# A fused attention and feed-forward kernel: part of the first v on a second queue, and the second batch's q and k loaded and transposed earlier

## The chip, the cores and the metric

The kernel runs on one core of one Trainium2 chip. The metric is device time in microseconds (us); lower is better. Before the change the median of three runs is 308.27 us (307.86 to 308.33). The profile shown here is of one execution that took 307.91 us, of which 306.1 us lie between its first and its last instruction. TensorE's granted clock was 1.000 throughout.

## What is computed

Sliding-window attention for 8 batches of 8 heads, sequence length 576, head dimension 64, then a feed-forward layer over all 4608 tokens with a quadratic-linear activation (smelu). Cut to what matters:

```python
def _attn_ref(q, k, v):                       # q, k, v: (8, 8, 576, 64) fp32
    scores = 1/sqrt(64) * q @ k^T
    scores = where(abs(i - j) <= 32, scores, -1e9)
    attn = softmax(scores)
    return attn @ v

def _moe_ref(x, w_in, w_out):                 # x (4608, 512), w_in (512, 2048), w_out (2048, 512)
    h = x @ w_in
    g = where(h >= 1, h, where(h <= -1, 0, (h + 1)**2 / 4))
    return g @ w_out                          # (4608, 512) fp32

x = attn_out.transpose(0, 2, 1, 3).reshape(4608, 512)
return _moe_ref(x, w_in, w_out)
```

## The kernel before

The program is one long list of **slots** `a`. Slot `a` projects 256 tokens through 256 columns of `w_in` (eight matmuls into the PSUM tile `hp`), and evaluates the activation into `gT`. Eight slots make one block of 256 tokens. Around the slots lie the products of finished blocks with `w_out` (`pair` for the first blocks, `unit` later) and the attention of the batch that comes next: transposes of q and k, scores, `exp`, sums and normalisation into `xT`. Each slot's order on the engines is the order in which the program issues it:

```python
for a in range(NF * NB + 2 * NF):
    eng = None if a < 14 else V
    post = [] if a >= 40 else [x for n, x in pairs if n == a] + [a - NF] * (a >= 2 * NF + 2)
    ...
    hps = [pool.tile([128, 2, TB], FP, name="hp", tag=tag)]
    project(hps[0], f, r0, [(j, kk) for j in range(2) for kk in (0, 2, 1, 3)], True, True)
    ...
    rr = ewp.tile([128, 2, TB], FP, name="rr")
    A.activation(rr, hp, AF.Relu, scale=0.5, bias=0.5)
    mx = ewp.tile([128, 2, TB], FP, name="mx")
    if a in two_on_act:                       # two operations on ScalarE, one on VectorE
        A.activation(mx, rr, AF.Square)
        V.scalar_tensor_tensor(g, hp, 1.0, mx, op0=ALU.max, op1=ALU.min)
    else:                                     # one on ScalarE, two on VectorE
        V.tensor_max(mx, hp, rr)
        V.scalar_tensor_tensor(g, rr, 1.0, mx, op0=ALU.min, op1=ALU.mult)
    flush()                                   # the multiplications that normalise sums
    run(a)                                    # what at(a, ...) has put there
    for x in post:
        pair(x)                               # or unit
    ...
    run(a + 0.5)
```

`ewp` has three buffers for each name, so the `mx` of slot `a` uses the buffer of slot `a - 3`. `hp` has two PSUM buffers; slot 6 alone takes one from another pool.

What is planned for the first slots:

```python
pairs = [(6, 0), (7, 1), (8, 2), (9, 3), (11, 4), (12, 5), (15, 6), (15, 8), (16, 7), (17, 9)]
two_on_act = (1, 7, 8, 9, 10, 11, 12)
at(1, (tposes, 0, (0, 1), (1, 1)))                     # first batch, second half of q and k
at(2, (scores, 0, (0, 1), (0, 2), (2, 4)), (scores8, 0, ps_o))
at(3, (scores, 0, (1, 2), (0, 2), (2, 4), ps_n), (sums, 0, 0, TB, MAIN, ps_s))
at(4, (sums, 0, 1, TB, MAIN))
at(5, (sums, 0, 0, MAIN, S, ps_s))
at(13, seq[0][1])                                      # second batch, scores
at(13.5, (*seq[1][1], ps_n))
at(14, (*seq[0][0], ps_s), seq[1][0])                  # second batch, sums
...
for t in range(2):
    at(11 + t, (tposes, 1, (t, 0), (t, 1)))            # second batch, q and then k
```

`pair(x)` multiplies a quarter of the inner dimension of `w_out` (`g = x % 4`) for 256 output columns; `x` 0 to 3 therefore need the four quarters of `w_out` in turn.

The transposes of one `tposes` call go to two PSUM buffers, and the copies out of them are shared between two engines:

```python
def tposes(b, *sets):
    todo = []
    for (t, half), pool in zip(sets, (ps_s, ps_n)):
        tp = pool.tile([128, 2, 8, 128], BF, name="tp", tag="bb")
        todo += [tpose(b, 2 * half + part, t, (A.copy, V.tensor_copy)[part], tp[:, part]) for part in range(2)]
    for copy in todo:
        copy()
```

All inputs but the very first q are loaded by the GpSimd queue, which turns fp32 into bf16 on the way. v comes in rows of one head and token, 64 numbers. A tile of v holds 18 **chunks** of 64 tokens for each of four pairs of heads (nine of one head and nine of the next), and is loaded by four transfers:

```python
def load_v(b, n):
    ...
    nc.gpsimd.dma_start(out=vn[b][64 * a:64 * a + 64, :, h], in_=v[b, y:y + 2]
                        .rearrange("y s d -> (y s) d").rearrange("(c r) d -> r c d", r=64))
```

The order of the loads: first q (sync and ScalarE queues), then on the GpSimd queue the first half of k, v, and

```python
cuts = [0, 256, 512, 768, 1024, 1280, 1792, DFF]
w = [(load_w_in, c0, c1, h) for c0, c1 in zip(cuts, cuts[1:]) for h in range(2)]
put(w[:4] + [(load_half, 1, t, h) for t in range(2) for h in range(2)] + w[4:12])
put([(load_w_out, 0, 0, 4)] + w[12:])
put([(load_w_out, 0, k, k + 4) for k in range(4, 16, 4)] + [(load_rows, 1, t) for t in range(2)])
put([(load_v, 1, n) for n in range(4)])
...
put([(load_w_out, 1, 8 * n, 8 * n + 8) for n in range(2)])
put([(load_nat, 2, t) for t in range(2)] + [(load_v, 2, n) for n in range(4)])
```

Eight such transfers can be under way at once; each further one waits for the one issued eight before it.

Of the kernel before, what the change touches and what calls it, by code (L numbers as in the profile page):

```python
# [7 lines left out]
FP = mybir.dt.float32  # L8
# [6 lines left out]
def kernel(  # L15
# [19 lines left out]
    nc = tc.nc  # L35
    B, H, S, D = q.shape
    NT, DM, DFF = out.shape[0], 512, 2048
    NY = H // 2
    NC = S // 64
# [4 lines left out]
    PAD = 32  # L44
    WIDE = 72, 136
    LONG = 2

    const = ctx.enter_context(tc.tile_pool(name="const", bufs=1))
    nat = ctx.enter_context(tc.tile_pool(name="nat", bufs=2))
# [3 lines left out]
    ewp = ctx.enter_context(tc.tile_pool(name="ewp", bufs=3))  # L53
    osp = ctx.enter_context(tc.tile_pool(name="osp", bufs=3))
    ps_h = ctx.enter_context(tc.tile_pool(name="ps_h", bufs=2, space=bass.MemoryType.PSUM))
    ps_s = ctx.enter_context(tc.tile_pool(name="ps_s", bufs=1, space=bass.MemoryType.PSUM))
    ps_n = ctx.enter_context(tc.tile_pool(name="ps_n", bufs=1, space=bass.MemoryType.PSUM))
# [17 lines left out]
    V, P, A = nc.vector, nc.gpsimd, nc.scalar  # L75


    qn, kn, vn = {}, {}, {}
# [20 lines left out]
            nc.gpsimd.dma_start(out=x[:, :, h], in_=src[b, NY * h:NY * h + NY].rearrange("y s d -> (y s) d")  # L99
                                .rearrange("(u p) d -> p u d", p=128))  # L100

    def load_v(b, n):
        if b not in vn:
            vn[b] = nat.tile([128, 2 * NC, 2, D], BF, name="vn", tag="vn", bufs=3)
        h, a = divmod(n, 2)
        y = NY * h + 2 * a
        nc.gpsimd.dma_start(out=vn[b][64 * a:64 * a + 64, :, h], in_=v[b, y:y + 2].rearrange("y s d -> (y s) d")  # L107
                            .rearrange("(c r) d -> r c d", r=64))

    def load_w_in(c0, c1, h):  # L110
        nc.gpsimd.dma_start(out=w_in[64 * h:64 * h + 64, :, c0:c1],  # L111
# [32 lines left out]
    def put(todo):  # L144
        for fn, *x in todo:
            fn(*x)
# [2 lines left out]
    w = [(load_w_in, c0, c1, h) for c0, c1 in zip(cuts, cuts[1:]) for h in range(2)]  # L149
    put(w[:4] + [(load_half, 1, t, h) for t in range(2) for h in range(2)] + w[4:12])  # L150
    put([(load_w_out, 0, 0, 4)] + w[12:])
    put([(load_w_out, 0, k, k + 4) for k in range(4, 16, 4)] + [(load_rows, 1, t) for t in range(2)])
    put([(load_v, 1, n) for n in range(4)])
    P.tensor_copy(band[HD[1], 0:128], band[HD[1], 64:192])
    for m, n, x in ((mask4, 8, 128), (mask8, 4, TAIL)):
# [8 lines left out]
    def qkT(b, t):  # L164
        if t == 0:
            return qTs[b % 3][:, PAD:]
        if b not in kT:
            kT[b] = ktp.tile([128, NY * S], BF, name="kT")
        return kT[b]

    def tpose(b, n, t, copy, ps):


        half, part = divmod(n, 2)
        j0, j1 = ((0, 5), (5, 9))[part]
        if b:
            src = qn[b] if t == 0 else kn[b]
            src = [src[:, half + 2 * h] for h in range(2)]
            dst = qkT(b, t).rearrange("d (y e p j) -> d y e p j", y=2, e=2, j=9)[:, half, :, :, j0:j1]
            like = "d j (e p) -> d e p j"  # L180
        else:
            src = (qn, kn)[t][b, half]
            src = src if src.shape[1] == 9 else [src[:, h] for h in range(2)]
            dst = qkT(b, t).rearrange("d (y l p j) -> d l y p j", l=2, p=32, j=9)[:, half, :, :, j0:j1]
            like = "d j (p y) -> d y p j"
        for j in range(j0, j1):
            if isinstance(src, list):
                for h in range(2):
                    nc.tensor.transpose(ps[HD[h], j - j0], src[h][:, D * j:D * j + D], ident)  # L189
            else:  # L190
                nc.tensor.transpose(ps[:, j - j0], src[:, j], ident)
        return lambda: copy(dst, ps[:, :j1 - j0].rearrange(like, p=64 if b else 32))
# [120 lines left out]
    def flush():  # L313
        while muls:
            muls.pop(0)()


    TB = 256
# [6 lines left out]
    def tposes(b, *sets):  # L325

        todo = []
        for (t, half), pool in zip(sets, (ps_s, ps_n)):
            tp = pool.tile([128, 2, 8, 128], BF, name="tp", tag="bb")
            todo += [tpose(b, 2 * half + part, t, (A.copy, V.tensor_copy)[part], tp[:, part]) for part in range(2)]  # L330
        for copy in todo:
            copy()

# [14 lines left out]
    with tc.tile_pool(name="ps_p", bufs=1, space=bass.MemoryType.PSUM) as ps_p:  # L348
        keep_warm(11, ps_h, "hp")

        V.memset(qkT(0, 0).rearrange("d (y s) -> d y s", y=NY)[:, :, S // 2:352], 0.0)
        for b in range(LONG):
            V.memset(qkT(b, 0).rearrange("d (y s) -> d y s", y=NY)[:, :, S - PAD:], 0.0)
# [24 lines left out]

    NB = NT // TB
    NF = DFF // 256  # L380
    pairs = [(6, 0), (7, 1), (8, 2), (9, 3), (11, 4), (12, 5), (15, 6), (15, 8), (16, 7), (17, 9)]
    two_on_act = (1, 7, 8, 9, 10, 11, 12)
    ev = {}

    def at(a, *todo):


        ev.setdefault(a, []).extend(x for x in todo if x)

    def steps(b, cut):  # L390

        for k, (lo, hi) in enumerate(((0, cut), (cut, MAIN))):
            for y1 in range(2):
                yield (sums, b, y1, lo, hi), (scores, b, (y1, y1 + 1), (0, 2), (2 * k, 2 * k + 2))
        yield (sums, b, 0, MAIN, S), (scores8, b)
# [4 lines left out]
    at(4, (sums, 0, 1, TB, MAIN))  # L400
    at(5, (sums, 0, 0, MAIN, S, ps_s))
    seq = [x for b in range(1, B) for x in steps(b, 224)]
    at(13, seq[0][1])
    at(13.5, (*seq[1][1], ps_n))
    at(14, (*seq[0][0], ps_s), seq[1][0])
    at(16, seq[2][1])
    for n, a in enumerate((18, 20, 26.5, 28)):
# [5 lines left out]
    for n, a in enumerate(sl):  # L413
        at(a, seq[6 + n][0], seq[7 + n][1] if n < len(sl) - 1 else None)
    for t in range(2):
        at(11 + t, (tposes, 1, (t, 0), (t, 1)))
    loads, xps = {}, {16: [(2, 0)], 18: [(2, 1)]}
    for b in range(LONG + 1, B):
        a = sl[5 * (b - 1) - 7] - 17
# [7 lines left out]
    def home(t):  # L427

        return (3 - t % 4 if t % 4 in (0, 3) else t % 4) if WIDE[0] <= NF * t < WIDE[1] else t % 4
# [43 lines left out]
    def run(pos):  # L473
        todo = []
        for fn, *x in ev.get(pos, []):
            if fn is sums:
                todo.append(sums(*x))
            elif fn is tposes:
                tposes(*x)
            else:  # L480
                pool = (x.pop(),) if x[-1] in (ps_s, ps_n, ps_o) else ()
                fn(*x, eng, *pool)
        for end in todo:
            end()
# [10 lines left out]
    for a in range(NF * NB + 2 * NF):  # L495
        wide = WIDE[0] <= a < WIDE[1]
        eng = None if a < 14 else V
        post = [] if a >= 40 else [x for n, x in pairs if n == a] + [a - NF] * (a >= 2 * NF + 2)
        for b, x in loads.get(a, []):
            if x < 2:  # L500
                load_nat(b, x)
            else:
                for n in range(4):
                    load_v(b, n)
        if a == 0 or a > 3:
            flush()
        if a < NF * NB:
            if wide:
                n, f = divmod(a - WIDE[0], 2 * NF)
                t = WIDE[0] // NF + 2 * n  # L510
                r0 = TB * t % RING
                hp = ps_h.tile([128, 2, TB], FP, name="hp", tag="hp")
                for n, kk in enumerate((0, 2, 1, 3)):
                    nc.tensor.matmul(hp.rearrange("p n t -> p (n t)"), w_in[:, kk, 128 * f:128 * f + 128],  # L514
                                     xT[:, kk, r0:r0 + 2 * TB], start=n == 0, stop=n == 3)
                g = gT[:, f, home(t):home(t + 1) + 1:home(t + 1) - home(t)]
            else:
                t, f = divmod(a, NF)
                r0 = TB * t % RING
                if a in (0,):  # L520
                    hps = [ps_h.tile([128, 2, TB], FP, name="hp", tag="hp") for _ in range(2)]
                    for y in range(2):
                        for n in range(2):
                            project(hps[n], f + n, r0, [(j, y + 2 * m) for j in range(2) for m in range(2)], y == 0, y == 1)
                elif not hps:
                    pool, tag = (ps_o, "op") if a == 6 else (ps_h, "hp")
                    hps = [pool.tile([128, 2, TB], FP, name="hp", tag=tag)]
                    project(hps[0], f, r0, [(j, kk) for j in range(2) for kk in (0, 2, 1, 3)], True, True)
                hp = hps.pop(0)
                g = gT[:, 2 * f:2 * f + 2, home(t)]  # L530

            rr = ewp.tile([128, 2, TB], FP, name="rr")
            A.activation(rr, hp, AF.Relu, scale=0.5, bias=0.5)  # L533
            mx = ewp.tile([128, 2, TB], FP, name="mx")
            if a in two_on_act:
                A.activation(mx, rr, AF.Square)
                V.scalar_tensor_tensor(g, hp, 1.0, mx, op0=ALU.max, op1=ALU.min)
            else:
                V.tensor_max(mx, hp, rr)  # L539
                V.scalar_tensor_tensor(g, rr, 1.0, mx, op0=ALU.min, op1=ALU.mult)  # L540
        flush()
        run(a)
        for x in post:
            if x < 16:
                pair(x)
            else:
                for j in range(4):
                    unit(4 * x + j)
        if a >= 40:
            n = (4, 3, 3)[a % 3] if a < 88 else 4  # L550
            for x in range(done, done + n):
                unit(x)
            done += n
        run(a + 0.5)
        for x in xps.get(a, []):
            xpose(*x)

# [29 lines left out]
```

The softmax here doesn't subtract the row's maximum and nothing guards it: scores larger than these inputs give would overflow.

## Time and profile before

| | |
|---|---|
| Time, median of 3 runs | 308.27 us |
| Span of the profiled execution | 306.1 us |
| TensorE (PE) busy | 298.4 us |
| TensorE idle up to 44 us | 4.35 us |
| VectorE (DVE) busy, ScalarE (ACT) busy | 239.6 us, 191.2 us |
| Bytes moved by DMA | 35.67 MB, 117 GB/s on average |

In the time-ordered rows below, the first number is the start in us from the beginning of the span, the second is how long the row lasted, then come engine, source line, operation, and output<-inputs with partitions x elements. "x8" means that eight instructions are merged in the row. What stands in brackets at the end is how long the engine had been idle before the row and what released it. PEld is TensorE's weight load, which overlaps its matmuls. A row of POOL with the operation DMA_DIRECT2D is GpSimd writing the descriptors of a transfer, not the transfer itself. In a list of waits, the numbers after the colon are the total, how often, and the longest.

The projections start at the following times (slot: us): 0: 13.24, 2: 18.53, 3: 20.23, 4: 22.18, 5: 23.84, 6: 25.23, 7: 26.99, 8: 28.73, 9: 30.48, 10: 32.23, 11: 33.59, 12: 36.57, 13: 39.55, 14: 41.78, 15: 43.93. A projection takes 0.87 us where others follow it without a gap, as does one `pair`; a set of transposes takes 1.12.

### The profile page before, as it was taken

How to read it: one execution, taken by the hardware profiler on the slowest of the kernel's cores; microseconds unless marked ns; L12 is line 12 of the kernel's file. 1: busy time of each engine (PE TensorE's matmuls, PEld its weight loads, DVE VectorE, ACT ScalarE, POOL GpSimd, SP SyncE). 2: the span in 40 equal slices, each digit the busy share in tenths (PEclk: the TensorE clock that was granted, in tenths of full speed). 3: DMA queues.
4: the chain of work that ended last, by engine and by line, in shares of the span. 5: the costliest groups of instructions: out<-in, count | busy, mean ns of one | idle time of the engine just before them, and what ended most of it. 6: DMA issues, size and time to landing. Idle time of an engine off the chain costs nothing.

```text
span 306.1 us, 7974 instructions
## 1 busy us (share of the span) xinstructions
PE 298.4 (97%) x3388; PEld 181.2 (59%) x3388; DVE 239.6 (78%) x376; ACT 191.2 (62%) x320; POOL 77.1 (25%) x92
## 2 busy tenths in 40 slices
PE   8889999999999999999999999999999999999995
PEld 3468878876666676666654544444445444446644
DVE  3268568888888989998999998888888888788700
ACT  3688896748856856776766766665667654444311
POOL 8787661037009009004600900000000000000000
PEclk9999999999999999999999999999999999999999
DMA  9999999999999999999998991550101000000121
GB/s 153 184 197 198 186 196 153 173 156 164 139 186 109 181 169 124 165 144 116 148 127 166 145 156 39 111 115 34 36 34 37 36 34 35 36 34 34 59 80 69
DMA packets 137171, 35.67 MB, mean 117 GB/s; under 512 B 122160, under 2 KB 132912, under 8 KB 137136
## 3 DMA queue, kind: packets, MB, share of 16 engines
q0 software_dynamic: 102976, 18.06, 83.5%
q1 hardware_dynamic: 34016, 16.81, 26.1%
q8 instruction: 26, 0.43, 0.6%
q10 hardware_dynamic: 144, 0.29, 0.3%
q14 instruction: 9, 0.07, 0.1%
HBM read 36.70 MB, written 9.44 MB: 151 GB/s over the span
## 4 chain that ended last, share of the span: by engine, by line
PE 91%; POOL 3%; DMA 2%; ACT 1%; issue 1%; DVE 0%; POOLq 0%; ACTq 0%
PE op L449 36%; PE hp L489 22%; PE hp L514 18%; PE bb L295 6%; PE op L464 4%; PE bb L229 2%; DMA w_in<-in_moe_w_in_dram 2%; POOL vn L107 1%; PE op L440 1%; POOL w_in L111 1%; PE tp L189 1%; ACT pt L237 1%; POOL kh L86 1%; POOL qh L86 0%; PE bb L208 0%
## 5 line engine op out<-in xcount | busy, mean ns | idle before, releaser
L533 ACT ACTIVATE rr<-hp 128x512 f32<-128x512 f32 x144 | 85.5, 595 | 86.1 <-PE hp L514 41.7
L449 PE MATMUL op<-w_out,gT 128*128 128x512 bf16 x496 | 126.9, 380 | 0.0
L539 DVE TENSOR_TENSOR mx<-hp,rr 128x512 f32<-128x512 f32 x137 | 94.4, 689 | 26.1 <-ACT rr L533 24.3
L540 DVE SCALAR_TENSOR_TENSOR gT<-rr,mx 128x512 bf16<-128x512 f32 x137 | 94.8, 692 | 4.7
L489 PE MATMUL hp<-xT,w_in 128*128 128x256 bf16 x640 | 83.1, 273 | 2.2 <-DMA w_in<-in_moe_w_in_dram 1.4
L489 PEld LDWEIGHTS <-w_in 128*128 128x128 bf16 x640 | 61.8, 98 | 22.7 <-issue 2.8
L449 PEld LDWEIGHTS <-gT 128*128 128x128 bf16 x496 | 46.1, 98 | 45.2
L514 PE MATMUL hp<-xT,w_in 128*128 128x512 bf16 x256 | 65.7, 379 | 0.0
L514 PEld LDWEIGHTS <-w_in 128*128 128x128 bf16 x256 | 25.0, 98 | 30.2
L99 POOL DMA_DIRECT2D qn<-in_q_dram x12 | 14.6, 1224 | 89.5 <-DMA kT<-kn 87.4
L237 ACT ACTIVATE pt<-bb 128x1024 bf16<-128x1024 f32 (+1 forms) x33 | 32.7, 1001 | 4.5 <-PE bb L229 3.1
L107 POOL DMA_DIRECT2D vn<-in_v_dram x32 | 27.7, 900 | 4.8 <-DMA w_out<-in_moe_w_out_dram 4.0
L307 DVE TENSOR_TENSOR xT<-bb,rc 128x512 bf16<-128x512 f32 (+1 forms) x32 | 21.0, 657 | 9.6 <-ACT rc L302 8.7
L453 ACT COPY osb<-op 128x512 f32<-128x512 f32 x31 | 18.0, 580 | 11.4 <-PE op L449 11.1
L302 ACT ACTIVATE rc<-lr 128x512 f32<-128x512 f32 (+2 forms) x40 | 23.5, 587 | 1.3
L301 ACT ACTIVATE lr<-bb 128x512 f32<-128x512 f32 (+2 forms) x40 | 22.1, 552 | 0.3 <-PE bb L295 0.3
L203 DVE TENSOR_TENSOR pt<-pt,mask 128x1024 bf16<-128x1024 bf16 (+1 forms) x33 | 20.3, 614 | 0.5 <-ACT pt L237 0.5
L295 PE MATMUL bb<-pt,ones 64*64 64x256 bf16 (+3 forms) x352 | 19.6, 255 | 0.1
L295 PE MATMUL bb<-pt,vn 64*64 64x128 bf16 (+3 forms) x712 | 18.4, 204 | 0.1
L295 PEld LDWEIGHTS <-ones 64*64 64x64 bf16 x352 | 10.3, 105 | 11.6 <-issue 11.6
L295 PEld LDWEIGHTS <-vn 64*64 64x64 bf16 x712 | 16.7, 107 | 0.3 <-DMA vn<-in_v_dram 0.3
L464 PE MATMUL op<-w_out,gT 128*128 128x256 bf16 x128 | 16.5, 273 | 0.0
(61 smaller groups left out, 140.3 us busy)
## 6 DMA issues: line engine op xcount, KB each, us to landing
out_dram<-osb SPq DMA_DIRECT2D x35, 256.0 KB, 2.3
vn<-in_v_dram POOLq DMA_DIRECT2D x32, 144.0 KB, 9.7
qn<-in_q_dram POOLq DMA_DIRECT2D x12, 288.0 KB, 6.2
kn<-in_k_dram POOLq DMA_DIRECT2D x12, 288.0 KB, 9.0
w_in<-in_moe_w_in_dram POOLq DMA_DIRECT2D x12, 128.0 KB, 5.6
w_out<-in_moe_w_out_dram POOLq DMA_DIRECT2D x4, 256.0 KB, 8.0
w_out<-in_moe_w_out_dram POOLq DMA_DIRECT2D x2, 512.0 KB, 13.2
kh<-in_k_dram POOLq DMA_DIRECT2D x4, 144.0 KB, 5.4
```

The lines of the kernel that those rows point to most:

```text
L107: nc.gpsimd.dma_start(out=vn[b][64 * a:64 * a + 64, :, h], in_=v[b, y:y + 2].rearrange("y s d -> (y s) d") .rearrange("(c r) d -> r c d", ...
L237: A.activation(p, ps[:, :, :w * n].rearrange(like, y=m), AF.Exp, scale=D ** -0.5)
L295: nc.tensor.matmul(bb[HD[h], a, o + c0:o + c1], ones[HD[a]] if c is None else vn[b][HD[a], c, h], p(a, h), start=n == 0, stop=True, skip_g ...
L301: A.activation(lr[:, :, :D0], bb[:, :, D0:2 * D0], AF.Ln)
L302: A.activation(rc[:, :, :D0], lr[:, :, :D0], AF.Exp, scale=-1.0)
L449: nc.tensor.matmul(op[tt], gT[:, j, home(tt // 2), 128 * (tt % 2):128 * (tt % 2) + 128], w_out[:, j], start=j == 0, stop=j == 15)
L464: nc.tensor.matmul(o[:, tt], gT[:, j, p, 128 * tt:128 * tt + 128], w_out[:, j, 256 * half:256 * half + 256], start=not done, stop=len(done ...
L489: nc.tensor.matmul(hp[:, j], w_in[:, kk, 256 * f + 128 * j:256 * f + 128 * j + 128], xT[:, kk, r0:r0 + TB], start=first and n == 0, stop=l ...
L514: nc.tensor.matmul(hp.rearrange("p n t -> p (n t)"), w_in[:, kk, 128 * f:128 * f + 128], xT[:, kk, r0:r0 + 2 * TB], start=n == 0, stop=n == 3)
L533: A.activation(rr, hp, AF.Relu, scale=0.5, bias=0.5)
L539: V.tensor_max(mx, hp, rr)
L540: V.scalar_tensor_tensor(g, rr, 1.0, mx, op0=ALU.min, op1=ALU.mult)
```

## The change

Three things are altered.

1. For the first batch only, 14 of the 18 chunks of v come by the four first transfers. The other four (the last tokens of every second head) come later by the sync queue, in fp32, into a buffer borrowed from `mx`, and VectorE casts them into the tile of v after slot 3. The aim is that k, w_in and what else stands behind v in the queue comes sooner; slots 0 and 1 don't use the four chunks.
2. The second batch's q and k are loaded ahead of the last quarter of `w_out`. They are transposed in slots 10 and 11 (after the products of slot 11) instead of 11 and 12, and the scores move from 13 and 13.5 to 12.5 and 13. The one `pair` that uses that last quarter moves from slot 9 to slot 13.
3. In every `tposes` call ScalarE now copies both parts of the first set, and VectorE both parts of the second. Slot 8's activation takes one operation on ScalarE and two on VectorE.

```diff
+    VC = NC + 5
...
-    def load_v(b, n):
+    def load_v(b, n, late=None):
...
-        nc.gpsimd.dma_start(out=vn[b][64 * a:64 * a + 64, :, h], in_=v[b, y:y + 2].rearrange("y s d -> (y s) d")
-                            .rearrange("(c r) d -> r c d", r=64))
+        x = v[b, y:y + 2].rearrange("y s d -> (y s) d").rearrange("(c r) d -> r c d", r=64)
+        if b:
+            nc.gpsimd.dma_start(out=vn[b][64 * a:64 * a + 64, :, h], in_=x)
+        elif late is None:
+            nc.gpsimd.dma_start(out=vn[b][64 * a:64 * a + 64, :VC, h], in_=x[:, :VC])
+        else:
+            nc.sync.dma_start(out=late[64 * a:64 * a + 64, h], in_=x[:, VC:])
...
-    put([(load_w_out, 0, k, k + 4) for k in range(4, 16, 4)] + [(load_rows, 1, t) for t in range(2)])
+    put([(load_w_out, 0, k, k + 4) for k in (4, 8)] + [(load_rows, 1, t) for t in range(2)] + [(load_w_out, 0, 12, 16)])
...
-        for (t, half), pool in zip(sets, (ps_s, ps_n)):
+        for (t, half), pool, copy in zip(sets, (ps_s, ps_n), (A.copy, V.tensor_copy)):
...
-            todo += [tpose(b, 2 * half + part, t, (A.copy, V.tensor_copy)[part], tp[:, part]) for part in range(2)]
+            todo += [tpose(b, 2 * half + part, t, copy, tp[:, part]) for part in range(2)]
...
-    pairs = [(6, 0), (7, 1), (8, 2), (9, 3), (11, 4), (12, 5), (15, 6), (15, 8), (16, 7), (17, 9)]
-    two_on_act = (1, 7, 8, 9, 10, 11, 12)
+    pairs = [(6, 0), (7, 1), (8, 2), (11, 4), (12, 5), (13, 3), (15, 6), (15, 8), (16, 7), (17, 9)]
+    two_on_act = (1, 7, 9, 10, 11, 12)
...
-    at(13, seq[0][1])
-    at(13.5, (*seq[1][1], ps_n))
+    at(12.5, seq[0][1])
+    at(13, (*seq[1][1], ps_n))
...
-        at(11 + t, (tposes, 1, (t, 0), (t, 1)))
+        at(10 + 1.5 * t, (tposes, 1, (t, 0), (t, 1)))
...
-            mx = ewp.tile([128, 2, TB], FP, name="mx")
+            mx = ewp.tile([128, 2, TB], FP, name="mx", tag="mx")
...
+        if a == 2:
+            late = ewp.tile([128, 2, 2 * NC - VC, D], FP, name="late", tag="mx")
+            for n in range(4):
+                load_v(0, n, late)
+        if a == 3:
+            V.tensor_copy(vn[0][:, VC:].rearrange("p c h d -> p h c d"), late)
```

## The prediction, made before the changed kernel was run

> **What bounds the kernel now.** I read the page's busy shares and chain first, then TensorE's waits, then the time-ordered list of instructions for the first 45 us, because every edit falls there.
>
> ```profile
> PE 298.4 (97%) x3388; PEld 181.2 (59%) x3388; DVE 239.6 (78%) x376; ACT 191.2 (62%) x320; POOL 77.1 (25%) x92
> ...
> PE 91%; POOL 3%; DMA 2%; ACT 1%; issue 1%; DVE 0%; POOLq 0%; ACTq 0%
> ```
>
> TensorE works for 298.4 of 306.1 us and is 91% of the chain. Only its 7.7 us of idle time can be won, plus delays hidden inside groups of matmuls. A table of 2 us windows puts 4.35 us of that idle time before 44 us, and the last window, 250 to 306, holds 3.27. In between there is almost nothing. TensorE's own waits say what the early part consists of:
>
> ```profile
> PE hp L489 <- DMA w_in<-in_moe_w_in_dram: 1.4, 2, 0.7
> ...
> PE tp L189 <- DMA kh<-in_k_dram: 0.5, 1, 0.5
> PE hp L489 <- DVE xT L307: 0.4, 1, 0.4
> PE hp L489 <- DVE gT L537: 0.3, 1, 0.3
> ```
>
> The columns are total us, times, longest. The transfers cost 1.9 us: at 14.50 (w_in), 17.12 (second half of k) and 18.53 (w_in). The 0.3 is at 33.59, slot 10 to 11, where ScalarE does two operations per slot.
>
> The GpSimd rows show when transfers land: a new one is issued only when an older one has landed, so an issue that waited dates a landing.
>
> ```profile
> 22.74 0.74 POOL L93 DMA_DIRECT2D qn<-in_q_dram  x1 [0.42 <-DMA w_in<-in_moe_w_in_dram]
> 23.99 0.74 POOL L93 DMA_DIRECT2D kn<-in_k_dram  x1 [0.50 <-DMA w_in<-in_moe_w_in_dram]
> ...
> 33.62 1.21 POOL L99 DMA_DIRECT2D qn<-in_q_dram  x1 [0.38 <-DMA qn<-in_q_dram]
> 36.47 1.21 POOL L99 DMA_DIRECT2D qn<-in_q_dram  x1 [1.64 <-DMA kn<-in_k_dram]
> ```
>
> So the two pieces of w_in columns 1280 to 1792 landed at 22.7 and 23.95, the second batch's q at 33.6, its k at 36.4. Against that stands TensorE's demand:
>
> ```profile
> 22.90 0.69 DVE L540 SCALAR_TENSOR_TENSOR gT<-rr,mx 128x512 bf16<-128x512 f32 x1
> ...
> 23.28 0.27 PE L295 MATMUL bb<-pt,vn 64*64 64x96 bf16 x8
> ...
> 23.84 1.03 PE L489 MATMUL hp<-xT,w_in 128*128 128x256 bf16 x8
> ...
> 33.59 1.03 PE L489 MATMUL hp<-xT,w_in 128*128 128x256 bf16 x8 [0.33 <-DVE gT L537]
> 34.55 1.20 PE L189 MATMUL tp<-ident,qn 128*64 128x128 bf16 x36
> ...
> 40.75 0.65 PE L229 MATMUL bb<-qT,kT 64*64 64x128 bf16 x16
> 41.41 0.44 PE L229 MATMUL bb<-qT,kT 64*64 64x128 bf16 x16
> ```
>
> The projection at 23.84 uses the w_in that landed at about that moment: behind a TensorE that looks busy, the DMA queue sets nearly the same pace up to slot 5. At 40.75 the same 16 matmuls take 0.65 instead of 0.44: 0.2 us of waiting for kT inside a group. The sums of slot 14 have another gap of 0.2 (43.11 to 43.44).
>
> **What the Trainium skill says.** "DMA: Bandwidth & Descriptors", Specifications: a transfer needs pieces of 512 B for line rate. v is written in rows of 128 B; the trace agrees: 150 GB/s at 8 to 10 us, where v is in flight, and 193 to 205 from 10 to 20 us with mostly w_in. The same page, "Queues, rings and completion order": each DMA engine serves its queues in turn. So the late v on the sync queue should share the engines with w_in rather than come free; the trace before has no such mixture on its own. "VectorE: DVE Perf Modes", the section on mode 2x_2P: a copy out of SBUF handles two fp32 elements a cycle. The 640-element cast below agrees: 640 / 2 / 0.96 GHz is 0.33 us, and it took 0.43.
>
> ```profile
> 4.84 0.43 DVE L344 CAST qb<-q 128x640 bf16<-128x640 f32 x1
> ```
>
> **The change part by part.**
>
> *1. Four of v's 18 chunks leave the first transfers.* v is 4 x 144 KB; it streams from about 6.8 us (k's first half in) to 10.66 (TensorE's wait for v ends), 3.9 us. 4/18 of that is 0.87 us, by which everything behind it lands earlier. On TensorE's path: the 0.3 us wait for v at 10.66 goes, so ln, exp and the multiplication come 0.27 earlier (ScalarE is busy with exp until 10.93, so no more). The second xT is then ready at 14.21 instead of 14.48. The slot 1 projection no longer waits for w_in (14.5 minus 0.87 is 13.65), so its first four matmuls are done before 14.21 and only eight (0.87 us) follow instead of twelve: slots 0 and 1 end about 0.7 us earlier. The k transposes and the w_in of slot 2 move by 0.87 with their transfers. Slot 2 starts about **0.7 us earlier**.
>
> *2. The four chunks come back on the sync queue.* 4 transfers of 64 KB fp32, issued when the buffer of slot 0's mx is free, at 17.62 minus 0.7, about 16.9. With some 0.5 us per issue (an output of 128 rows takes 0.34, these have 256 pieces) and 2 to 3 us to land (outputs: 2.3; the first q: 3.2 to 3.9), they are in at about 22. They are 1,024 row pieces, as many as they were, so I give them the same 0.87 us of the engines. By slot 5 the queue is where it was: w_in at 23.9. **The 0.7 is then gone**, at the w_in of slot 5.
>
> *3. One cast on VectorE.* 512 elements: 0.27 + 0.1 = 0.37 us, an estimate from the row above. It stands after slot 3's gT, which ends at 23.59 minus 0.7 = 22.9, so it ends at about 23.3. Only the third group of slot 4's sums needs it, which TensorE reaches at 23.35 minus 0.7 = 22.65. That is a **new wait of 0.6 to 0.7 us**, which uses up the same 0.7: it and the w_in of slot 5 overlap and are not added. Slot 5 starts as before, 23.8 +- 0.3.
>
> *4. q and k ahead of w_out's last quarter.* q to k took 2.85 us for 576 KB, so 256 KB is 1.27 us. q lands at 32.3 and k at 35.15. The half-group of w_out products that needs the last quarter goes from slot 9 to 13, where it has long landed (36.4).
>
> *5. Slots 9 to 13.* TensorE's work is the same, in another order. Slot 8's evaluation goes to VectorE, sparing ScalarE 0.63 us. Slot 9 is 0.87, ending at 31.36; slot 10's projection 31.36 to 32.23; the q transposes from 32.35 (q just landed), 1.12 long; slot 11's projection at 33.5, its buffer free (slot 9's gT at 33.5). Then w_out products to 35.3, and k transposes: the first half at once, the second only when VectorE has copied both q pieces of its buffer (about 36.2), some 0.3 us of waiting. Slot 12 and its products until 38.5; scores then wait for kT on VectorE until about 38.8. Slot 13's projection, the other scores and the moved products end near 41.3, where slot 14 starts. Before, it started at 41.78. That is **0.45 us** less. The scores are now two slots' work away from the sums, so the 0.2 gap in slot 14 goes: **0.65 to 0.7 us in all**.
>
> After slot 14 the order is the old one, and 260 us are bound by TensorE at full clock; a lead of 0.7 is neither enlarged nor lost. 308.27 - 0.7 = **307.6 us**.
>
> **Rivals.** *A: the start's gain stays.* If the two queues together move more than one alone, w_in is not late in slot 5; the cast's wait still takes most, and q, landing at about 32, holds slot 10. At most 0.5 more: 307.0. For it: at 38 to 40 us the engines moved 220 GB/s; against: the steady 193 to 205 while w_in streams look like a limit. *B: the late v is really late.* If it lands at 24 instead of 22, VectorE stands still with it, TensorE waits one us longer in slot 4, and the new order wins back 0.7 at most: 308.3 to 308.6. For it: small pieces in a full queue, where GpSimd's v loads take 9.7 us to land (median). *C: q or k arrives too late for the earlier slots.* q now has no slack (0.97 before). If the late v costs the engines more than the 0.87 saved, q, k and all before shift with it; 0.5 us more eats the gain: about 308.1. *D: all this is hidden*, since TensorE fills the time: 308.3. Against it: the 33.59, 40.75 and 43.44 gaps are TensorE's own.
>
> **Range and chances.** The sum is 0.7 us gained, A reaches 1.3 and B loses 0.3; the three runs before differ by 0.5. Hence 306.7 to 308.4. 2% is 6.2 us; all of TensorE's idle time before 44 us is 4.35. Faster or slower by over 2% would need something outside the first 45 us.
>
> **What would show it.** Right, if the profile after has slot 2's projection near 17.8, a TensorE wait of about 0.6 for the late cast in slot 4, slot 5 at 23.8, no 0.33 wait at slot 11, and slot 14 starting near 41.1 to 41.4. Step 2 is wrong if slot 5 starts before 23.4; step 3 if TensorE doesn't wait for VectorE in slot 4; step 4 if the q transposes wait for DMA. A sum outside the range would mean a cost of the sync queue's small transfers that I have not seen, or a stall in the rearranged copies.

## The result and the profile after

The changed kernel takes **313.34 us** (median of 5, 312.93 to 314.51) against 308.27: the ratio is 1.0176, 95% interval 1.0154 to 1.0199. By the medians it is 5.1 us slower, where 0.7 us less was predicted.

The profiled execution took 314.51 us, the longest of the five, with a span of 312.7. First its page: busy shares, then TensorE's busy tenths and granted clock in 40 slices of 7.8 us.

```profile
PE 296.1 (95%) x3350; PEld 182.9 (58%) x3388; DVE 241.7 (77%) x378; ACT 191.0 (61%) x319; POOL 76.6 (24%) x92
...
PE   8884999999999999999999999999999999999995
...
PEclk9997899999999999999999999999999999999999
```

Before, the slices from the fourth on were full and the clock 9 throughout. Now the fourth slice has a hole, and the clock is low in the fourth and fifth. Everything after looks as it did. Stretches of 2 us show the hole (columns: busy time and instructions of each engine; then the clock, the DMA share and GB/s):

```profile
22.00:24.00 2.00, 0.91 (x14) 0.48 (x12) 0.97 (x2) 1.97 (x4) 0.55 (x2) 1.00 1.33 180
24.00:26.00 2.00, 0.00 (x0) 0.00 (x0) 0.00 (x0) 0.01 (x1) 0.95 (x2) 1.00 1.39 187
26.00:28.00 2.00, 0.01 (x4) 0.02 (x4) 0.65 (x2) 0.00 (x0) 1.69 (x3) 0.87 1.45 196
28.00:30.00 2.00, 2.00 (x27) 1.51 (x28) 1.75 (x3) 1.12 (x2) 1.47 (x3) 0.50 1.28 206
30.00:32.00 2.00, 2.00 (x36) 1.28 (x35) 1.40 (x3) 1.25 (x3) 1.94 (x4) 0.50 1.23 213
32.00:34.00 2.00, 2.00 (x11) 1.45 (x10) 1.39 (x3) 0.96 (x2) 1.43 (x2) 0.50 1.21 201
```

From 24 to 27 us TensorE, VectorE and ScalarE all stand still while the DMA engines move data at the usual rate. Then TensorE is busy, but at half its clock. TensorE's rows in time order, from slot 4 to slot 7, say who waits for whom:

```profile
21.60 1.05 PE L495 MATMUL hp<-xT,w_in 128*128 128x256 bf16 x8
...
27.98 0.32 PE L301 MATMUL bb<-pt,vn 64*64 64x128 bf16 x4 [5.08 <-DVE vn L566]
...
28.64 1.89 PE L495 MATMUL hp<-xT,w_in 128*128 128x256 bf16 x8
...
31.14 1.89 PE L495 MATMUL hp<-xT,w_in 128*128 128x256 bf16 x8
...
34.43 1.04 PE L495 MATMUL hp<-xT,w_in 128*128 128x256 bf16 x8
```

And VectorE's row of the cast:

```profile
27.35 0.58 DVE L566 CAST vn<-late 128x512 bf16<-128x512 f32 x1 [4.34 <-DMA late<-in_v_dram]
```

TensorE waits 5.08 us in slot 4's sums for VectorE's cast, and the cast 4.34 us for the late v. The same eight matmuls then take 1.89 instead of 1.04 us. The late transfers themselves, by the answer for their tile:

```profile
L114 SPq DMA_DIRECT2D late<-in_v_dram x4: 610/636/677, 17.1 to 19.2; - x4
...
DMA to landing us min/median/max: 6.8/7.5/8.1
```

They were issued from 17.1 to 19.2 us, where about 16.9 had been predicted for the first, and took 6.8 to 8.1 us to land instead of 2 to 3.

Slot by slot, after minus before (from the projections' starts): slot 2 -0.96, slot 4 -0.58, slot 5 +4.80, slot 7 +7.44, slot 9 +7.44, slot 14 +7.24, slot 15 +6.91; the span +6.6. So the lead at the start is there, the wait costs 5.4 up to slot 5 (with some 0.3 of half clock in slot 4's last sums), the half clock of slots 5 and 6 another 2.6, and slots 8 to 15 win back 0.5.

One execution fixes slot 5 to about 1 us only: in the four profiles of kernels that load the whole first v up front (before, reordering only, and the two with extra transfers in part 3) it starts at 23.84, 24.65, 23.98 and 24.71, as its `w_in` lands.

### The profile page after: what moved, and what is told of

Read it like the earlier page. It is cut to its first block, busy times and chain, and to the rows that moved or that the text cites. A ratio compares the mean times of both kernels' runs of the same rounds, so it can differ in the third digit from the quotient of the medians.

```text
span 312.7 us, 7946 instructions
## 1 busy us (share of the span) xinstructions
PE 296.1 (95%) x3350; PEld 182.9 (58%) x3388; DVE 241.7 (77%) x378; ACT 191.0 (61%) x319; POOL 76.6 (24%) x92
## 4 chain that ended last, share of the span: by engine, by line
PE 90%; DMA 3%; ACT 2%; issue 2%; DVE 2%; SPq 1%; DVEq 0%; ACTq 0%
PE op L455 34%; PE hp L495 22%; PE hp L520 18%; PE bb L301 6%; PE op L470 5%; DMA late<-in_v_dram 3%; PE bb L235 2%; PE z L344 2%; PE op L446 1%; ACT pt L243 1%; SPq L114 1%; PE tp L195 0%; ACT rc L308 0%; ACT rr L539 0%; ACT lr L307 0%
## 5 line engine op out<-in xcount | busy, mean ns | idle before, releaser
L455 PE MATMUL op<-w_out,gT 128*128 128x512 bf16 x460 | 119.5, 379 | 5.0 <-issue 4.8
L495 PE MATMUL hp<-xT,w_in 128*128 128x256 bf16 x640 | 84.6, 276 | 1.2 <-DMA w_in<-in_moe_w_in_dram 0.7
L520 PE MATMUL hp<-xT,w_in 128*128 128x512 bf16 x256 | 65.7, 379 | 0.0
L110 POOL DMA_DIRECT2D vn<-in_v_dram x28 | 24.0, 894 | 4.4 <-DMA w_out<-in_moe_w_out_dram 3.6
L301 PEld LDWEIGHTS <-vn 64*64 64x64 bf16 x712 | 17.1, 110 | 5.3 <-DVE vn L566 5.3
L470 PE MATMUL op<-w_out,gT 128*128 128x256 bf16 x128 | 17.2, 281 | 0.0
```

Source lines behind the costliest of these rows:

```text
L301: nc.tensor.matmul(bb[HD[h], a, o + c0:o + c1], ones[HD[a]] if c is None else vn[b][HD[a], c, h], p(a, h), start=n == 0, stop=True, skip_g ...
L455: nc.tensor.matmul(op[tt], gT[:, j, home(tt // 2), 128 * (tt % 2):128 * (tt % 2) + 128], w_out[:, j], start=j == 0, stop=j == 15)
L470: nc.tensor.matmul(o[:, tt], gT[:, j, p, 128 * tt:128 * tt + 128], w_out[:, j, 256 * half:256 * half + 256], start=not done, stop=len(done ...
L495: nc.tensor.matmul(hp[:, j], w_in[:, kk, 256 * f + 128 * j:256 * f + 128 * j + 128], xT[:, kk, r0:r0 + TB], start=first and n == 0, stop=l ...
```

## Experiments

**The theory after the result.** The late v, slowed by sharing the DMA engines with the GpSimd queue, is the whole loss, first by the wait and then by the clock. Rivals: the reordering costs as well; the slow slots come from other waits than the clock; sync transfers of small pieces are slow by themselves.

| kernel | median us | ratio to before, 95% interval |
|---|---|---|
| changed kernel | 313.34 | 1.0176 (1.0154 to 1.0199) |
| reordering only | 307.89 | 0.9987 (0.9979 to 0.9996) |
| late v only | 314.43 | 1.0199 (1.0177 to 1.0220) |
| dummy matmuls in the wait | 311.11 | 1.0096 (1.0081 to 1.0111) |
| two late chunks | 310.31 | 1.0057 (1.0035 to 1.0079) |
| late v in pieces of 1 KB | 310.36 | 1.0073 (1.0054 to 1.0093) |
| late v by the GpSimd queue | 310.30 | 1.0069 (1.0042 to 1.0096) |
| late v issued at the start | 308.08 | 1.0003 (0.9990 to 1.0017) |
| late v left out | 307.05 | 0.9958 (0.9944 to 0.9972) |

**1. Reordering only, and late v only.** The first puts the whole v back on the GpSimd queue:

```diff
-            nc.gpsimd.dma_start(out=vn[b][64 * a:64 * a + 64, :VC, h], in_=x[:, :VC])
+            nc.gpsimd.dma_start(out=vn[b][64 * a:64 * a + 64, :, h], in_=x)
...
-        if a == 2: ...                        # late, its four loads
-        if a == 3: ...                        # and the cast
```

> The whole v comes by the GpSimd queue again, nothing by the sync queue; q and k ahead, the copies and the moved products stay as in the changed kernel. Theory: the late v alone made the loss, and the reordering gains its 0.4 to 0.7 us: 307.6 to 307.9 us, and no TensorE wait for a cast. Rival: the earlier transposes wait for q's transfer or for the copies, and cost something of their own: 308.5 us or more, with a DMA or copy wait on TensorE near slots 10 to 12.

The second keeps the late v and its cast, and has the loads, `pairs`, `two_on_act`, scores, transposes and copies of the kernel before.

> Only the late four chunks and their cast are added to the kernel before; loads, slots and copies after that in the old order. Theory: the whole loss is here: 313.5 to 314.0 us (the changed kernel's 313.3 plus what the reordering gains), with one wait of TensorE for the cast of about 5 us. Rival (the reordering costs too): below 313 us.

Reordering alone is 0.4 us faster than before, the late v alone 6.1 us slower. Its TensorE wait is 5.3 us, and its 314.43 us lie 0.4 above the expected range. The two add up to 5.7, near the 5.1 of the changed kernel with runs that scatter by 1.5. The rival that the reordering costs falls. Reordering alone also beats both kernels; from slot 8's projection to slot 15's it takes 14.66 us (29.54 to 44.20) where the kernel before took 15.20. The late v's wait, then slots 8 and 15 of the reordering:

```profile
28.06 0.32 PE L301 MATMUL bb<-pt,vn 64*64 64x128 bf16 x4 [5.30 <-DVE vn L566]
```

```profile
29.54 1.04 PE L495 MATMUL hp<-xT,w_in 128*128 128x256 bf16 x8
...
44.20 1.05 PE L495 MATMUL hp<-xT,w_in 128*128 128x256 bf16 x8
```

**2. TensorE kept busy in the wait.** The late v is as late as ever; 22 matmuls on zeros fill the time.

```diff
         flush()
+        if a == 4:
+            keep_warm(22, ps_o, "op")
         run(a)
```

> The changed kernel with 22 matmuls on zeros (128x512, 0.22 us each at full clock) put ahead of slot 4's sums, so that TensorE works while it would wait for the late v. The late v lands as before. Theory: the loss is 5.1 us of standing still plus 2.6 us of half clock afterwards; the clock now stays at 1.0, slots 5 to 8 take their usual time, and the run takes 310.5 to 311 us. Rival: the slow slots 5 to 8 come from other waits (buffers, w_in), not from the clock: no more than 0.5 us are gained.

TensorE in this run, in time order:

```profile
22.49 4.91 PE L344 MATMUL z<-warm 128*128 128x512 bf16 x22
...
27.96 0.25 PE L301 MATMUL bb<-pt,vn 64*64 64x128 bf16 x4 [0.29 <-DVE vn L568]
...
28.36 1.05 PE L495 MATMUL hp<-xT,w_in 128*128 128x256 bf16 x8
...
29.75 1.05 PE L495 MATMUL hp<-xT,w_in 128*128 128x256 bf16 x8
```

The cast comes at the same time, yet slots 5 to 9 take 6.64 us (28.36 to 35.00), as they did before (23.84 to 30.48), where the changed kernel needs 9.28 (28.64 to 37.92). The mean granted clock is 1.000 instead of 0.989, and the run is 2.2 us faster than the changed kernel. The clock is a cost of its own, about 2.2 of the 5.1 us by the medians. The 311.11 us lie slightly above the expected 310.5 to 311.

**3. What makes the late v late.** First the same four transfers where the GpSimd queue is empty; they go into a buffer of their own, and their cast is not used.

```diff
+        if a == 110:
+            late = const.tile([128, 2, 2 * NC - VC, D], FP, name="late")
+            for n in range(4): ...            # the four sync loads of the changed kernel
...                                           # a cast in slot 116 that nothing uses
```

> The kernel before, plus the same four transfers of late v (256 pieces of 256 B each) on the sync queue in slot 110, where the GpSimd queue is empty and only outputs are written; nothing uses them but a cast in slot 116. If it was the sharing with the GpSimd queue that made them slow, they land 2 to 3 us after issue. If small pieces from the sync queue are slow by themselves, they land 5 us or more after issue here too. Time: within 0.5 us of the kernel before.

One execution: 307.8 us, and for the tile:

```profile
L561 SPq DMA_DIRECT2D late<-in_v_dram x4: 610/614/660, 224.0 to 226.4; - x4
...
DMA to landing us min/median/max: 2.3/2.3/2.4
```

Alone they land in 2.3 us, a third of the time. They are not slow by themselves; it is the company. What in it decides, pieces, bytes or a fixed delay? Half as many chunks, and then the same bytes in larger pieces:

```diff
-    VC = NC + 5
+    VC = NC + 7
```

> Two late chunks instead of four: half the pieces and half the bytes on the sync queue (4 transfers of 128 pieces of 256 B). If the landing time grows with pieces or with bytes, it halves: from 6.8 to 8.1 us down to 3.4 to 4, landing at about 22.5; TensorE waits 1 us or less, the clock stays up, and the run takes 307.5 to 308.5 us. If the landing time is a fixed delay behind the filled GpSimd queue, it stays at 6.8 to 8 us and the run at 312 us or more.

```diff
-            nc.sync.dma_start(out=late[64 * a:64 * a + 64, h], in_=x[:, VC:])
+            z = v[b, y:y + 2].rearrange("y s d -> (y s) d")[64 * VC:].rearrange("(r c) d -> r (c d)", r=64)
+            nc.sync.dma_start(out=late[64 * a:64 * a + 64, h].rearrange("r c d -> r (c d)"), in_=z)
```

> The late four chunks in pieces of 1 KB: each partition takes four neighbouring tokens in one piece, so the same 256 KB come in 256 pieces instead of 1,024. (The tokens of these chunks then lie in another order, so the output differs there; the work is the same.) If each piece waits for its turn against the GpSimd queue, the time to land falls to a third or less, 2.5 us, the late v is in by 22, and the run takes about 307.5 to 308.2 us. If bytes decide, or a fixed delay, it stays at 6.8 to 8 us and 313 us.

Times to land, first of the two late chunks, then of the four in 1 KB pieces:

```profile
DMA to landing us min/median/max: 5.6/6.2/6.6
```

```profile
DMA to landing us min/median/max: 5.6/6.0/6.6
```

Both expectations fail in the middle. By the medians of one execution each, 512 pieces take 6.2 us, 256 larger ones with twice the bytes 6.0, and 1,024 took 7.5. Bytes hardly count there. Pieces do, but, as an estimate from these three, about 5 us would be left at none. TensorE waits 2.3 us in both profiles, and even that halves the clock: in the first from about 25.4 to 28.8 us, in the second from about 26.5 to 29.9. First the two late chunks, then the 1 KB pieces, where slot 5 still runs at full clock:

```profile
25.45 0.27 PE L301 MATMUL bb<-pt,vn 64*64 64x64 bf16 x4 [2.27 <-DVE vn L566]
25.65 1.89 PE L495 MATMUL hp<-xT,w_in 128*128 128x256 bf16 x8
```

```profile
25.16 0.25 PE L302 MATMUL bb<-pt,vn 64*64 64x128 bf16 x4 [2.28 <-DVE vn L567]
...
25.55 1.05 PE L496 MATMUL hp<-xT,w_in 128*128 128x256 bf16 x8
...
27.21 1.89 PE L496 MATMUL hp<-xT,w_in 128*128 128x256 bf16 x8
```

Then probes of 16 KB, 64 pieces, released at the end of five slots of the kernel before:

```diff
+        if a in (2, 5, 8, 20, 110):
+            probe[a] = const.tile([64, D], FP, name=f"probe{a}")
+            V.memset(probe[a], 0.0)
+            nc.sync.dma_start(out=probe[a], in_=v[0, 0, 64:128])
...                                           # casts of the probes in slot 116
```

> The kernel before with five single transfers of 16 KB (64 pieces of 256 B[...]) on the sync queue, each released by a small VectorE memset at the end of slots 2, 5, 8, 20 and 110. If a sync transfer takes turns with the GpSimd queue piece by piece, so few pieces land in 2.3 to 3 us everywhere. If it must wait for all that the GpSimd queue has under way, it lands in 2 to 2.3 us in slot 110 and, about as late as the GpSimd loads issued at the same time, in 5 us in slot 2, and 6 us or more in slots 5 and 8. Time: within 0.7 us of the kernel before.

One execution, 308.7 us. The probe of slot 5 (window 26 to 29 us) and that of slot 110:

```profile
L559 SPq DMA_DIRECT2D probe<-in_v_dram x1: 471/471/471, 28.2 to 28.2; - x1
...
DMA to landing us min/median/max: 5.0/5.0/5.0
```

```profile
L559 SPq DMA_DIRECT2D probe<-in_v_dram x1: 496/496/496, 231.0 to 231.0; - x1
DMA to landing us min/median/max: 2.9/2.9/2.9
```

The five take 5.2, 5.0 and 6.0 us under load (slots 2, 5, 8) and 2.7 and 2.9 later. Neither alternative holds. GpSimd loads issued from 26 to 32 us took 12 to 13, so a sync transfer does not stand at the end of that line. But neither does a small one pass quickly: two to three us are added even to 64 pieces, and about 1.5 to 2.5 more for 1,024. Bytes in flight alone don't do it: while the probe of slot 20 was under way (65.7 to 68.4 us) the engines moved 271 GB/s, all by the hardware queues (the sync queue's own outputs among them), and it landed in 2.7 us; at slot 5 they moved 206 GB/s, 1.00 of 1.03 MB by the GpSimd queue, and it took 5.0. So the company of the GpSimd queue's loads goes with the late landing, but how it acts is not settled: no run here separates the engine's turns from the memory's answer to that many reads.

**4. Other places for the same four chunks.** On the GpSimd queue, behind w_in's columns 1024 to 1280, cast on the way:

```diff
-    put(w[:4] + [(load_half, 1, t, h) for t in range(2) for h in range(2)] + w[4:12])
+    put(w[:4] + [(load_half, 1, t, h) for t in range(2) for h in range(2)] + w[4:10]
+        + [(load_v, 0, n, True) for n in range(4)] + w[10:12])
...                                           # load_v's late branch on the GpSimd queue; no buffer, no cast
```

> The late four chunks by the GpSimd queue, cast on the way, behind w_in's columns 1024 to 1280; no buffer, no VectorE cast; the rest as in the changed kernel. They land in order, at about 21 to 21.5, ahead of slot 4's sums at 22.7. Then slot 5 waits for w_in 1280 to 1792, put back to about 23.9 by them, so the start's gain is gone and the reordering's stays: 307.4 to 307.9 us. If the queue has spare time there, slot 5 starts earlier and it is 307.0.

A miss: 310.3 us (309.18 to 312.13). TensorE doesn't wait for v, but in slot 5 for w_in:

```profile
25.22 1.03 PE L496 MATMUL hp<-xT,w_in 128*128 128x256 bf16 x8 [1.94 <-DMA w_in<-in_moe_w_in_dram]
```

Slot 5's w_in was issued at 18.34 instead of 16.65. The last kernel below has the same start without the four chunks, and its slot 5 starts at 23.56: so, as an estimate from these two profiles, the chunks hold up what follows them by about 1.7 us (25.22 - 23.56, with the scatter at slot 5 of up to 0.9), about twice the 0.87 that the prediction took them to be worth. The profile shows the shortest of six executions, 309.18 us, in which the clock stayed at 1.000 in spite of the 1.94 us wait. In the other five the mean clock was 0.994 or 0.995, and they took 1.1 to 2.9 us longer. So the median of 310.3 includes a lower clock that this profile does not show.

On the sync queue at the very start, into a buffer of their own:

```diff
+    late = const.tile([128, 2, 2 * NC - VC, D], FP, name="late")
+    for n in range(4):
+        load_v(0, n, late)
     V.memset(ones, 1.0)
...                                           # and no loads after slot 2; the cast stays
```

> The late four chunks in a buffer of their own, issued on the sync queue right behind the first q instead of after slot 0. They then share the engines with k and v at 2 to 10 us. Whatever they wait, they are in by 15 us, long ahead of the cast, so TensorE's long wait and the half clock are gone. But they take their share of the queue from k and v: the start gains little or nothing on the kernel before, and the cast's place behind slot 3's evaluation still costs 0.6 us in slot 4: 307.5 to 308.3 us. If fast, it shows that only the time to land was wrong in the change, not its idea.

308.08 us, like the kernel before. Slot 4's wait for the cast is what the prediction's step 3 gave for a v that is in time:

```profile
24.58 0.25 PE L304 MATMUL bb<-pt,vn 64*64 64x128 bf16 x4 [0.49 <-DVE vn L565]
```

But slot 0's projection starts at 14.32, against 13.24 to 13.94 in the four kernels that load all of v up front: k and v share the engines with the four chunks, and the start is later, not earlier. The four transfers took 5.7 to 6.5 us to land there, so they are not quick at the start either; they only have time.

Last, the four chunks set to zero and never loaded:

```diff
+    V.memset(vn[0][:, VC:], 0.0)
...
-        if a == 2: ...                        # late, its four loads
-        if a == 3: ...                        # and the cast
```

> The changed kernel without the late transfers and without their cast: the four chunks are set to zero at the start (so the output differs for their tokens); k, w_in and the rest come earlier by what the four chunks took. It is the most that splitting v could bring if the late part were free. If w_in's place in the queue binds slot 5, slot 5 moves by 0.6 to 0.9 us, to 23.0 to 23.3, and the run takes 307.0 to 307.4 us, 0.5 to 0.9 less than reordering alone. If the start's lead is lost elsewhere (q's landing in slot 10, the copies), it takes 307.7 to 308.

307.05 us, about 0.9 less than reordering alone (from the two ratios), and in the expected range. Slot 5 was expected at 23.0 to 23.3; in this profile it starts at 23.56:

```profile
23.56 1.03 PE L496 MATMUL hp<-xT,w_in 128*128 128x256 bf16 x8 [0.65 <-DMA w_in<-in_moe_w_in_dram]
```

Slot 15 starts at 43.11, against 43.93 before. So a free late v would have been worth about 0.9 us; all three ways of really loading it lost at least that.

## Why the prediction was wrong

**Step 2 failed, in one term: "2 to 3 us to land".** Measured: 6.8 to 8.1. With it fell step 3's "new wait of 0.6 to 0.7 us", which was 5.08. I took the 2 to 3 us from the median of all outputs (2.3), most of which run when no loads are left, and from the first q (3.2 to 3.9), which runs when the loads have only begun. The trace before had a number near the right one. Outputs of the same sync queue (stores, so not quite the same thing), in the window 30 to 40 us, where there is a single one, and in 200 to 250 us:

```profile
L470 SPq DMA_DIRECT2D out_dram<-osb x1: 418/418/418, 33.3 to 33.3; - x1
...
DMA to landing us min/median/max: 7.4/7.4/7.4
```

```profile
DMA to landing us min/median/max: 2.0/2.0/2.4
```

A median over a run with two stages was used for the stage that was not in the majority. With 7.4 us in step 2's own sum (16.9, four issues of 0.5, then landing) the v would have been in at about 26.3, and a wait of about 4 us could have been read off.

**Rival B named the mechanism**, a late v that stops VectorE and TensorE, but gave it one us instead of 4.5, and nothing for what follows it. **The half clock was missing from every rival**; it cost 2.2 us, by the dummy matmuls. Rivals A and C did not show: the w_in of slot 5 came at 23.97, no earlier than before, and TensorE waited for neither q nor k. D falls with the 0.4 us of the reordering.

**The bound on a loss was wrong in kind.** The 4.35 us of TensorE's idle time limit what can be won, not what can be lost. The late v alone cost 2.0% (1.8 to 2.2), all of it before slot 8.

The other steps:

- Step 1 was about right: slot 2 at 17.57 (predicted 17.8), slot 4 0.58 earlier. The seven kernels that move chunks out of the first transfers and put nothing beside them start slot 2 at 17.34 to 17.98, the four that load all of v up front at 18.24 to 18.76. (14.5 minus 0.87 is 13.63, not 13.65; nothing hangs on it.)
- Step 2's second half, w_in of slot 5 back at 23.9: GpSimd's next issue, which waited for it, came at 23.97. True for the changed kernel, but nobody was waiting by then, and the same landing lay anywhere from 24.0 to 24.9 in the profiles with all of v up front, so the agreement is in part luck.
- Step 3's reasoning held: with v in time the wait is 0.49 where 0.6 to 0.7 was predicted. The cast of 512 elements took 0.42 to 0.64, not 0.37. (The 256 elements of the two late chunks took 0.29: so 0.13 us for 256 more, which is two a cycle, and about 0.16 that is fixed, where 0.1 had been estimated.)
- Step 4: k landed at about 35.4 with reordering alone (predicted 35.15), 36.1 in the changed kernel.
- Step 5 was slightly large, and its parts were the other way round: from slot 8 to slot 15 the profiles of both the changed kernel and reordering alone gain about 0.53 us against the predicted 0.65 to 0.7, of it 0.2 up to slot 14 (predicted 0.45) and 0.33 in slot 14 (predicted 0.2). The measured times gain 0.4.

## What to carry to other kernels

The time that a transfer takes to land must be read from the stage in which it will run, next to the queue that it will share the engines with; a median over the whole run tells of the stage with most transfers. A piece of data moved to "later" needs slack measured in that landing time, and a wait of TensorE is to be charged with the lower clock that can follow it as well as with itself. Where the DMA queue is as tight as the engine, moving bytes within the same stretch gains little: here only leaving them out did.

## What was not expected of the hardware

After 5.1 us of standing still TensorE's granted clock was 0.50 for about 6.8 us (from 27.5 to 34.3). The Trainium skill, "TensorE: Matmul & The Clock Gate", Part 1, says that the clock is halved after an idle window of about 3.4 us and restored after as long a busy one. The second half agrees: in the profiles the stretches at half clock lasted 3.4 or 6.8 us. The first does not: a wait of 2.3 us was enough (two late chunks, and 1 KB pieces), and with 1 KB pieces the clock fell only when TensorE had been at work again for 1.3 us. So the length of the wait alone does not tell.

Nor does the kernel. Of the 16 executions with 1 KB pieces three had a mean clock of 1.000 and took 308.85 to 309.51 us, nine had 0.994 (310.00 to 310.75), and four 0.989 (311.94 to 313.61). In the profiles of the runs above a mean of 0.994 goes with 3.4 us at half clock and 0.989 with 6.8. A median over such executions tells mostly which of the three is the most frequent.

A sync transfer of only 64 pieces took 5 to 6 us with the GpSimd queue full and 2.7 to 2.9 otherwise.
